# Attention and a two-layer feed-forward block on one core: other issue costs for SyncE in the planner, and a limit by due time on its second engines

## The chip, the cores and the metric

One core of a Trainium2 chip runs the whole program. The metric is the device time of one execution in microseconds (us); lower is better. The engines are PE (TensorE, matmuls), DVE (VectorE), ACT (ScalarE), POOL (GpSimd) and SP (SyncE, which here issues every DMA).

## The reference

Causal attention over 4 batches, 12 heads, 448 positions and head size 64, followed by two dense layers with an ELU between them. The weights arrive as 64-bit floats.

```python
scores = scale * np.matmul(q, k.transpose(0, 1, 3, 2))
scores = np.where(mask, -1000000000.0, scores)
attn = np.exp(scores - np.max(scores, axis=-1, keepdims=True))
attn = attn / (np.sum(attn, axis=-1, keepdims=True) + 1e-09)
x = np.matmul(attn, v)            # 1792 tokens x 768 after the heads are joined
h = x @ w_in                      # 768 -> 2048
g = np.where(h > 0.0, h, np.exp(np.minimum(h, 0.0)) - 1.0)
out = g @ w_out                   # 2048 -> 768
```

## The kernel before, in words

**Tiling.** Tokens are cut into four groups of 448 columns: position block c (112 positions) of each of the four batches. `layers(0)` and `layers(1)` compute the first dense layer for groups 0 and 1, `mixed_o(0)` the second layer for both, then `mixed_h` and `mixed_o(1)` the two layers for groups 2 and 3. The attention for group 1 (`attention(0)`) and for groups 2 and 3 (`attention(1)`) is woven into the first three of these. From `mixed_o(0)` on each matrix product is done as seven half-size products (numbered 1, 2, 6, 7, 4, 5, 3 in the order of `GROUPS`), each of whose operands are sums or differences of blocks: `halves` makes the activations' (products 6 and later, function `add`, L693), `mixed` the weights'. Each float32 operand goes to TensorE as a high and a low part, three matmuls for a product (`three`, L727 to L729): `hi_lo` makes the high part (ACT L685, or DVE L686 as a second engine) and the low part by a subtraction (L688: DVE, or POOL as a second engine).

**The planner.** Nothing is issued while the work is described. `plan.add` records each piece of work with its buffers, and one or more "ways": (engine, cost in us, function, whether it uses the SBUF port that DVE and POOL share). The first way is the preferred engine, any other is a second engine. PE work gets a due time as it is described; `Plan.run` carries due times back through successors and through the buffers that are to be reused. Then it simulates: at each step every ready piece offers a start time `s` on each of its ways, the engine with the earliest start takes, among its pieces that could start within 0.12 us of that, the one due first, and its function is called. A port piece on one of DVE and POOL starts only when the other's port piece has ended. A second engine is passed over if the first engine would finish the piece before it ends there plus `LEAST` = 0.8 us. So the order of instructions on each engine, and the choice between engines, is fixed before the kernel runs, by the costs in the code. On the chip each engine then works through its list in that order, waiting on semaphores.

**DMA.** Every DMA is a piece on SP. Its cost is its issue time, 0.36 us up to 128 "rows" and 0.57 us above (L313); its landing is reckoned from the end of the issue by size and `LANDS` = 3.2 us. Work that reads the data becomes ready then.

**Lines that the steps touch.** L668 stores converted weights, L638 loads 64-bit weights (`load64`, for w_in and for w_out), L483 loads v, L843 loads half-size weights (`raw_piece`), L398 stores reciprocals. L646, L650, L651, L654 and L657 convert 64-bit weights, L657 on POOL alone. L335 is the softmax's maximum on DVE (`nm`), L339 its exponential on ACT, L593 the transposes on PE that need it. L815 adds on DVE what PE has left in PSUM.

Of the kernel before, what the change touches and what calls it, by code (L numbers as in the profile page):

```python
# [11 lines left out]
U32 = mybir.dt.uint32  # L12
# [5 lines left out]
CP = 112  # L18
# [90 lines left out]
class Plan:  # L109
# [7 lines left out]

    LANDS = 3.2

    def __init__(self):  # L120
        self.works, self.cap = [], 1e9

# [27 lines left out]
    def run(self):  # L150
        for n, w in enumerate(self.works):
            w.n = n
        for w in reversed(self.works):
            cost = w.ways[0][1]
            lead = 2.0 * cost + 0.4 + (8.0 + 2.0 * w.size if w.size else 0.0)
            dues = [s.due - lead for s in w.succs]
            least = min(dues, default=1e9) - self.AHEAD
            for x in w.bufs:
                if x.ring and not x.ring.in_order:
                    if x.n + x.ring.places < len(x.ring.bufs_of):  # L160
                        dues.append(x.ring.bufs_of[x.n + x.ring.places].due - lead)
                dues += [max(o.due - lead, least if x.ring.long else -1e9) for o in x.after]
            if w.due is None:
                w.due = min([w.cap] + dues)
            for x in w.bufs:
                x.due = min(x.due, w.due)
            w.missing = len(w.preds)
        free, ported = {}, {}
        backlog = {}
        moved = 0.0  # L170
        ready = {w: 0.0 for w in self.works if not w.missing}
        todo = len(self.works)
        self.log = []
        self.done = []
        while todo:
            starts = {}
            for w, t in ready.items():
                skip = {}
                for b in w.bufs:
                    if not b.placed:  # L180
                        f = b.ring.free_at(b, skip.get(b.ring, 0))
                        skip[b.ring] = skip.get(b.ring, 0) + 1
                        if f is None:
                            t = None
                            break
                        t = max(t, f + self.HOP)
                if t is None:
                    continue
                for way, (eng, cost, _, port) in enumerate(w.ways):
                    s = max(t, free.get(eng, 0.0))  # L190
                    if port:
                        s = max([s] + [f for e, f in ported.items() if e != eng])
                    if way:
                        e0, c0 = w.ways[0][:2]
                        before = sum(
                            o.ways[0][1] for o, to in ready.items()
                            if o is not w and o.ways[0][0] == e0 and o.due < w.due and to <= s
                        )
                        if max(t, free.get(e0, 0.0)) + before + c0 < s + cost + self.LEAST:
                            continue  # L200
                    starts.setdefault(eng, []).append((s, w.due, w.n, way, w))
            assert starts, "no work can start"
            eng, cands = min(starts.items(), key=lambda kv: min(kv[1])[0])
            s0 = min(cands)[0]
            s, _, _, way, w = min((c for c in cands if c[0] <= s0 + 0.12), key=lambda c: (c[1], c[2]))
            _, cost, fn, port = w.ways[way]
            if port:
                ported[eng] = s + cost
            for b in w.bufs:
                if not b.placed:  # L210
                    b.placed = True
                    b.ring.order.append(b)
                    b()
            free[eng], w.eng = s + cost, eng
            if w.size:
                moved = max(moved, s + cost) + w.size
                w.end = moved + self.LANDS
            else:
                w.end = s + cost
            self.log.append((s, w.end, eng, w.due, cost))  # L220
            self.done.append(w)
            fn()
            del ready[w]
            todo -= 1
            for b in w.bufs:
                b.left -= 1
                b.end = max(b.end, w.end)
            for o in w.succs:
                o.missing -= 1
                if not o.missing:  # L230
                    o.ready = max(
                        p.end + (0.0 if p.eng == o.ways[0][0] and not p.size else self.HOP) for p in o.preds
                    )
                    ready[o] = o.ready

# [2 lines left out]
def attention_moe_kernel(ctx, tc, qk, v, w_in, w_out, out):  # L238
# [68 lines left out]
    def pool(n, fn, rate=2.3e-3):  # L307
        return ("POOL", 0.1 + rate * n, fn, True)

    def dma(kb, rows, fn, reads, writes, least=0.0, store=False):  # L310
        size = rows * (15.7 + 39.2 * kb / rows) / 16.0e3
        call = (lambda: fn(nc.sync)) if store else fn
        plan.add(("SP", 0.36 if rows <= 128 else 0.57, call, False), reads, writes, size=max(least, size))  # L313

# [161 lines left out]
    def loads_23(p, b):  # L478
        n = 2 * CP + S
        raw, hl, t = new("w", [P, n], name="qk"), new("w6", [P, 2, n], F32R, "qkhl"), new("v", [CP, 2, NCH, D])  # L480
        src = qk[b, 2 * p:2 * p + 2].rearrange("h d t s -> (h d) (t s)")[:, 2 * CP:]
        dma(n // 2, P, lambda: nc.sync.dma_start(out=raw(), in_=src), [], [raw])
        dma(224, CP, lambda: nc.sync.dma_start(out=t(), in_=v[b, p]), [], [t])  # L483
        hi_lo(lambda: hl()[:, 0], lambda: hl()[:, 1], raw, n, (hl, 0), (hl, 1), raw)
        done(raw)
        return [dict(
            reads=[hl], v=(t, lambda half, x: t()[:, half, x]), split=((0, 0), (0, 1), (1, 0)),
            q=lambda d, i, g=g: hl()[d, i, chunk(g)], k=lambda d, i, n: hl()[d, i, 2 * CP:2 * CP + n],
        ) for g in range(2)]
# [140 lines left out]
    def load64(key):  # L630
        r = words[key] = new("w6", [P, KT, P, 2], U32, "w64")
        if key[0] == "i":
            n, out, src = KT, lambda: r().rearrange("p k c w -> p k (c w)"), w_in[key[1]]
        else:
            x, n = key[2], 4
            out = lambda: r()[:, :n].rearrange("p (h k) c w -> p h k (c w)", h=2)
            src = w_out[key[1]].rearrange("p (h f) c -> p h f c", h=2)[:, :, 2 * x:2 * x + 2]
        dma(n * P, P, lambda: nc.sync.dma_start(out=out(), in_=src.bitcast(U32)), [], [r])  # L638

    def convert(key):  # L640
        r, w = words.pop(key), new("w", [P, KT, P])
        n = KT if key[0] == "i" else 4
        size = n * P
        low, high = (lambda: r()[:, :n, :, 0]), (lambda: r()[:, :n, :, 1])
        wf = lambda: w()[:, :n]
        plan.add(dve(size, lambda: nc.vector.tensor_scalar(  # L646
            wf(), f32(high()), MOST, -MOST, op0=ALU.min, op1=ALU.max
        ), 0.55e-3, 0.06, True), [(r, 1)], [w])

        plan.add(act(size, lambda: nc.scalar.activation(wf(), wf(), AF.Prelu, scale=REBIAS, alpha=2.0 ** 32), 0.09), [], [w])  # L650
        plan.add(dve(size, lambda: nc.vector.tensor_scalar(  # L651
            wf().bitcast(U32), wf().bitcast(U32), 3, None, op0=ALU.logical_shift_left
        ), 0.55e-3, 0.06, True), [], [w])
        plan.add(act(size, lambda: nc.scalar.activation(  # L654
            low().bitcast(I32), low(), AF.Copy, scale=2.0 ** -29
        ), 0.16), [], [(r, 0)])
        plan.add(pool(size, lambda: nc.gpsimd.tensor_tensor(  # L657
            out=wf().bitcast(I32), in0=wf().bitcast(I32), in1=low().bitcast(I32), op=ALU.add
        )), [(r, 0)], [w])
        if key[0] == "i":  # L660
            done(r)
            home, src = kin[key[1]], wf
        else:
            h = key[1] // HALF_E
            home = kout[key[1]].rearrange("p (h f) c -> p h f c", h=2)[:, h:, 2 * key[2]:2 * key[2] + 2]
            src = lambda: wf().rearrange("p (h f) c -> p h f c", h=2)[:, h:]
        k = kept[key] = Buf(None, lambda: home)
        dma(n * 64, P, lambda eng: eng.dma_start(out=home, in_=src()), [w], [k], store=True)  # L668
        return w if key[0] == "i" else (w, r)

    def fetch(f):
# [168 lines left out]

    def raw_piece(srcs, reads, dst):
        w = new("w", [P, KT, P])
        dma(KT * 64, 2 * P, lambda: nc.sync.dma_start(out=dst(w()), in_=srcs), reads, [w])  # L843
        return in_two(w, KT)

    GROUPS = ((1, 2), (6, 7, 4), (5, 3))
# [265 lines left out]
```

## Time and profile before

| | us |
|---|---|
| median of 3 runs | 625.55 (623.75 to 629.59) |
| profiled execution, its own time | 623.13 |
| span in the profile | 621.4 |
| PE busy | 600.4 (97%) |
| DVE busy | 508.5 (82%) |
| ACT busy | 425.9 (69%) |
| POOL busy | 163.2 (26%) |

Busy shares are means over the whole span. The time from the first to the last instruction is the span; the profiled execution's own time is 1.7 us longer. A line such as L688 belongs to a helper that many callers use; the tile names beside it (out<-in) tell them apart: `whl` are the weights' two parts, `ph`/`pl` the activations' parts in the half-size products, `G` the first layer's output, `u`, `s` and `t` intermediate rows, `nm` the softmax maximum.

### The profile page before, as it was taken

How to read it: one execution, taken by the hardware profiler on the slowest of the kernel's cores; microseconds unless marked ns; L12 is line 12 of the kernel's file. 1: busy time of each engine (PE TensorE's matmuls, PEld its weight loads, DVE VectorE, ACT ScalarE, POOL GpSimd, SP SyncE). 2: the span in 40 equal slices, each digit the busy share in tenths (PEclk: the TensorE clock that was granted, in tenths of full speed). 3: DMA queues.
4: the chain of work that ended last, by engine and by line, in shares of the span. 5: the costliest groups of instructions: out<-in, count | busy, mean ns of one | idle time of the engine just before them, and what ended most of it. 6: DMA issues, size and time to landing. Idle time of an engine off the chain costs nothing.

```text
span 621.4 us, 11699 instructions
## 1 busy us (share of the span) xinstructions
PE 600.4 (97%) x4056; PEld 514.9 (83%) x4056; DVE 508.5 (82%) x1126; ACT 425.9 (69%) x960; POOL 163.2 (26%) x116
## 2 busy tenths in 40 slices
PE   5999999998999999999999999999999999999997
PEld 5655688877788888788788878999999889999996
DVE  4897788689998998989998798597678999998611
ACT  6988889878899989786688684365446765573300
POOL 0235532144343445242220610030001352010000
PEclk9999999998999999999999999999999999999999
DMA  9999999877999999888868598864332343352111
GB/s 218 292 355 360 386 287 271 230 224 247 297 342 344 372 308 300 282 266 261 260 214 268 195 291 243 240 171 127 107 116 84 101 126 104 104 151 69 39 51 45
DMA packets 114172, 135.95 MB, mean 219 GB/s; under 512 B 42560, under 2 KB 86848, under 8 KB 114112
## 3 DMA queue, kind: packets, MB, share of 16 engines
q1 hardware_dynamic: 114112, 135.20, 71.2%
q8 instruction: 32, 0.52, 0.4%
q14 instruction: 28, 0.23, 0.1%
HBM read 103.02 MB, written 32.15 MB: 218 GB/s over the span
## 4 chain that ended last, share of the span: by engine, by line
PE 56%; DVE 15%; ACT 10%; DMA 9%; issue 6%; POOL 2%; SPq 1%; POOLq 0%; DVEq 0%; ACTq 0%
PE op L727 9%; PE op L728 8%; PE op L729 8%; PE hp L727 6%; PE hp L729 5%; PE hp L728 5%; PE hp L749 5%; ACT a L339 4%; PE av L561 3%; PE sc L528 3%; DMA R<-rdram 3%; DMA w<-in_w_out 2%; DVE whl L688 2%; DVE a L335 2%; PE tr L593 2%
## 5 line engine op out<-in xcount | busy, mean ns | idle before, releaser
L685 ACT ACTIVATE whl<-w 128x768 fp32r<-128x768 f32 x90 | 75.6, 842 | 76.8 <-PE op L729 41.4
L727 PE MATMUL op<-ph,whl 128*128 128x448 f32 x336 | 126.6, 377 | 0.0
L728 PE MATMUL op<-pl,whl 128*128 128x448 f32 x336 | 122.8, 365 | 0.0
L729 PE MATMUL op<-ph,whl 128*128 128x448 f32 x336 | 122.7, 365 | 0.0
L688 DVE TENSOR_TENSOR whl<-w,whl 128x768 fp32r<-128x768 f32 x102 | 105.1, 1031 | 20.1 <-ACT whl L685 19.4
L339 ACT ACTIVATE a<-a,nm 112x448 f32<-112x448 f32 (+3 forms) x192 | 97.7, 520 | 28.4 <-DVE nm L335 27.9
L657 POOL TENSOR_TENSOR w<-w,w 128x512 int32<-128x512 int32 (+1 forms) x40 | 67.2, 1683 | 134.7 <-DVE w L651 76.5
L335 DVE CUSTOM_DVE_ANT_0 a<-sc,mask 112x448 f32<-112x448 f32 (+3 forms) x192 | 74.0, 442 | 11.9 <-PE sc L429 7.9
L727 PEld LDWEIGHTS op<-ph,whl 128*128 128x128 f32 x336 | 63.2, 188 | 8.6 <-issue 3.8
L729 PEld LDWEIGHTS op<-ph,whl 128*128 128x128 f32 x336 | 63.1, 188 | 5.1
L728 PEld LDWEIGHTS op<-pl,whl 128*128 128x128 f32 x336 | 63.3, 188 | 4.3
L727 PE MATMUL hp<-ph,whl 128*128 128x448 f32 x168 | 61.7, 367 | 1.4 <-DVE u L815 1.3
L729 PE MATMUL hp<-ph,whl 128*128 128x448 f32 x168 | 61.4, 365 | 0.0
L728 PE MATMUL hp<-pl,whl 128*128 128x448 f32 x168 | 61.3, 365 | 0.0
L597 ACT ACTIVATE at<-tr 112x448 f32<-112x448 f32 (+1 forms) x120 | 53.1, 496 | 5.9 <-PE tr L593 5.9
L727 PE MATMUL hp<-xh,whl 128*128 128x448 f32 x144 | 57.0, 396 | 0.0
L593 PE MATMUL tr<-ident,a 112*112 112x112 f32 x432 | 52.2, 262 | 4.3 <-DVE nm L335 4.3
L593 PEld LDWEIGHTS tr<-ident,a 112*112 112x112 f32 x432 | 45.8, 134 | 12.1 <-DVE nm L335 6.2
L729 PE MATMUL hp<-xh,whl 128*128 128x448 f32 x144 | 53.4, 371 | 0.9 <-DVE whl L688 0.8
L728 PE MATMUL hp<-xl,whl 128*128 128x448 f32 x144 | 53.1, 369 | 0.8 <-DVE xl L688 0.8
L561 PEld LDWEIGHTS av<-at,v 112*64 112x64 f32 x864 | 43.0, 137 | 12.1 <-ACT at L597 5.7
L561 PE MATMUL av<-at,v 112*64 112x112 f32 x864 | 50.9, 264 | 1.1 <-ACT at L597 0.8
(111 smaller groups left out, 1102.2 us busy)
## 6 DMA issues: line engine op xcount, KB each, us to landing
w<-kin SPq DMA_DIRECT2D x44, 384.0 KB, 5.8
w<-in_w_in SPq DMA_DIRECT2D x16, 768.0 KB, 8.3
w<-in_w_out SPq DMA_DIRECT2D x24, 512.0 KB, 6.7
w<-sout SPq DMA_DIRECT2D x32, 384.0 KB, 3.6
w<-kout SPq DMA_DIRECT2D x24, 384.0 KB, 4.5
qk<-in_qk SPq DMA_DIRECT2D x24, 336.0 KB, 5.9
kin<-w SPq DMA_DIRECT2D x16, 384.0 KB, 7.9
sout<-w SPq DMA_DIRECT2D x12, 512.0 KB, 6.9
```

The lines of the kernel that those rows point to most:

```text
L335: plan.add(dve(n, lambda: nc.vector.tensor_tensor_reduce(out=a()[:, c], in0=sc()[:, c], in1=mask[:, S - n:], op0=ALU.add, op1=ALU.min, sca ...
L339: plan.add(act(n, lambda: nc.scalar.activation(a()[:, c], a()[:, c], AF.Exp, bias=nm()[:, x:x + 1], scale=-1.0, accum_out=su()[:, x:x + 1] ...
L561: nc.tensor.matmul(av()[half_of(half), chunk(u % 4)], o["v"][1](half, i), at()[:, chunk(x)], start=i == 0, stop=i == chunks(u) - 1,)
L593: nc.tensor.transpose(tr()[:, chunk(x)], a[:, chunk(i)], ident)
L597: act(w, lambda: nc.scalar.activation(at()[:, :w], tr()[:, :w], AF.Copy)),
L657: plan.add(pool(size, lambda: nc.gpsimd.tensor_tensor(out=wf().bitcast(I32), in0=wf().bitcast(I32), in1=low().bitcast(I32), op=ALU.add)), ...
L685: act(n, lambda: nc.scalar.activation(h(), x(), AF.Copy), 0.09),
L688: sub = lambda eng: lambda: eng.tensor_tensor(out=l(), in0=x(), in1=f32(h()), op=ALU.subtract)
L727: nc.tensor.matmul(acc(), wh(k), xh(), start=first, stop=False, skip_group_check=more)
L728: nc.tensor.matmul(acc(), wh(k), xl(), start=False, stop=False, skip_group_check=more)
L729: nc.tensor.matmul(acc(), wl(k), xh(), start=False, stop=last, skip_group_check=more)
L749: pe(ONE, lambda: nc.tensor.matmul(hp(), w[0]()[:, k], x(), start=k == 0, stop=k == KT - 1), [*w, x], [hp], due)
```

## The change

The planner's cost of a DMA on SP becomes 0.48 us or 0.66 us, by a flag `long` (without it, more than 128 rows). Three callers set it so that a DMA of up to 128 rows counts as long (v at L483, w_out at L638, the stores of w_out's half at L668), and `raw_piece` so that one of 256 rows counts as short. Second engines get a new condition: a second engine isn't offered a piece of work that is due more than `SOON` = 20 us after the start it would have. One expression is broken into two lines.

```diff
+    SOON = 20.0
...
                     if port:
                         s = max([s] + [f for e, f in ported.items() if e != eng])
+                    if way and w.due > s + self.SOON:
+                        continue
                     if way:
...
-    def dma(kb, rows, fn, reads, writes, least=0.0, store=False):
+    def dma(kb, rows, fn, reads, writes, least=0.0, store=False, long=None):
         size = rows * (15.7 + 39.2 * kb / rows) / 16.0e3
         call = (lambda: fn(nc.sync)) if store else fn
-        plan.add(("SP", 0.36 if rows <= 128 else 0.57, call, False), reads, writes, size=max(least, size))
+        plan.add(("SP", 0.66 if (rows > P if long is None else long) else 0.48, call, False), reads, writes, size=max(least, size))
...
-        dma(224, CP, lambda: nc.sync.dma_start(out=t(), in_=v[b, p]), [], [t])
+        dma(224, CP, lambda: nc.sync.dma_start(out=t(), in_=v[b, p]), [], [t], long=True)
...
-        dma(n * P, P, lambda: nc.sync.dma_start(out=out(), in_=src.bitcast(U32)), [], [r])
+        dma(n * P, P, lambda: nc.sync.dma_start(out=out(), in_=src.bitcast(U32)), [], [r], long=key[0] == "o")
...
-        dma(n * 64, P, lambda eng: eng.dma_start(out=home, in_=src()), [w], [k], store=True)
+        dma(n * 64, P, lambda eng: eng.dma_start(out=home, in_=src()), [w], [k], store=True, long=key[0] == "o")
...
-        dma(KT * 64, 2 * P, lambda: nc.sync.dma_start(out=dst(w()), in_=srcs), reads, [w])
+        dma(KT * 64, 2 * P, lambda: nc.sync.dma_start(out=dst(w()), in_=srcs), reads, [w], long=False)
```

## Rows read from the trace of the kernel before

**Rows 1.** By stretch: busy us on PE, PEld, DVE, ACT, POOL; clock, DMA.
```profile
120.00:383.00 263.00, 255.91 (x2048) 218.33 (x2043) 238.97 (x532) 213.41 (x494) 95.16 (x65) 0.99 0.88 278
...
480.00:560.00 80.00, 78.60 (x387) 71.94 (x386) 78.25 (x121) 53.07 (x98) 21.53 (x15) 1.00 0.41 118
560.00:622.00 62.00, 57.07 (x282) 52.56 (x280) 26.51 (x43) 10.51 (x16) 0.00 (x0) 1.00 0.17 47
```

**Rows 2.** What PE waited for: total us, times, longest.
```profile
PE tr L593 <- DVE nm L335: 4.3, 4, 2.2
...
PE hp L727 <- DVE u L815: 1.3, 1, 1.3
PE hp L728 <- DVE xl L688: 0.8, 1, 0.8
PE av L561 <- ACT at L597: 0.8, 1, 0.8
PE hp L729 <- DVE whl L688: 0.8, 1, 0.8
```

**Rows 3.** PE in order of time: start, us, what [idle before <-releaser].
```profile
150.15 0.93 PE L593 MATMUL tr<-ident,a 112*112 112x112 f32 x6 [2.24 <-DVE nm L335]
```

**Rows 4.** The two stretches behind that idle time; columns as in rows 1.
```profile
150.00:152.00 2.00, 1.85 (x11) 1.49 (x12) 2.00 (x9) 1.87 (x7) 0.00 (x0) 0.80 1.07 311
152.00:156.00 4.00, 4.00 (x20) 3.50 (x21) 4.00 (x7) 3.23 (x9) 2.74 (x2) 0.67 0.86 270
```

**Rows 5.** DVE in order of time, ahead of that idle time's end.
```profile
145.87 1.38 DVE L688 TENSOR_TENSOR whl<-w,whl 128x768 fp32r<-128x768 f32 x1
147.17 1.37 DVE L693 TENSOR_TENSOR w<-w 128x256 f32<-128x256 f32 x1
148.57 0.43 DVE L693 TENSOR_TENSOR w<-w,w 128x256 f32<-128x256 f32 x1
```

**Rows 6.** POOL in order of time, the same stretch.
```profile
145.13 3.13 POOL L688 TENSOR_TENSOR pl<-G,ph 128x448 fp32r<-128x448 f32 x2
```

**Rows 7.** Line 727: duration min/median/max ns, first and last start us.
```profile
L727 PE MATMUL op<-ph,whl x336: 362/365/493, 244.5 to 616.3; 128*128 128x448 f32 x168
L727 PE MATMUL hp<-ph,whl x168: 362/365/472, 410.6 to 514.2; 128*128 128x448 f32 x168
```

**Rows 8.** Lines 688 and 693 on POOL: durations, first and last start, as rows 7.
```profile
L688 POOL TENSOR_TENSOR pl<-G,ph x10: 1140/1482/3059, 130.9 to 552.9; 128x448 fp32r<-128x448 f32 x10
...
L693 POOL TENSOR_TENSOR G<-G x9: 1142/1265/1873, 171.7 to 266.7; 128x448 f32<-128x448 f32 x9
L693 POOL TENSOR_TENSOR G<-u,G x6: 1154/1158/1802, 492.5 to 519.4; 128x448 f32<-128x448 f32 x6
L693 POOL TENSOR_TENSOR u<-u x4: 1167/1640/1748, 497.1 to 507.0; 128x448 f32<-128x448 f32 x4
```

**Rows 9.** Groups on DVE by shape: the same subtraction there.
```profile
L693 DVE TENSOR_TENSOR u<-u 128x448 f32<-128x448 f32 x4 | 2.5, 617 | 0.0
```

**Rows 10.** DVE in order of time, around PE's wait for u.
```profile
495.15 0.94 DVE L688 TENSOR_TENSOR whl<-w,whl 128x768 fp32r<-128x768 f32 x1
...
501.55 1.59 DVE L688 TENSOR_TENSOR whl<-w,whl 128x768 fp32r<-128x768 f32 x1
503.06 0.61 DVE L815 TENSOR_TENSOR u<-hp,u 128x448 f32<-128x448 f32 x1
```

**Rows 11.** POOL in order of time, the same stretch.
```profile
501.17 1.16 POOL L693 TENSOR_TENSOR G<-u,G 128x448 f32<-128x448 f32 x1 [1.43 <-DVE u L822]
502.40 1.74 POOL L693 TENSOR_TENSOR u<-u 128x448 f32<-128x448 f32 x1
```

**Rows 12.** SP's issues by line: duration min/median/max ns, first and last start.
```profile
L638 SPq DMA_DIRECT2D w<-in_w_out x24: 540/580/739, 81.6 to 217.6; - x24
L843 SPq DMA_DIRECT2D w<-sout x32: 319/320/598, 261.0 to 565.5; - x32
```

**Rows 13.** A wait of DVE for a DMA: total us, times, longest.
```profile
DVE w L646 <- DMA w<-in_w_out: 0.6, 1, 0.6
```

More of the change, by code (lines that the diff above doesn't have):

```diff
@@ L231, in run @@
                     o.ready = max(
-                        p.end + (0.0 if p.eng == o.ways[0][0] and not p.size else self.HOP) for p in o.preds
+                        p.end + (0.0 if p.eng == o.ways[0][0] and not p.size else self.HOP)
+                        for p in o.preds
                     )
```

## The prediction, made blind

> **What bounds the kernel now.** I read the busy time by stretch first. From 120 to 383 us PE is busy 255.91 of 263.00 us, from 480 to 560 us 78.60 of 80.00 [rows 1]: PE sets the time, its matmuls are the same in number after the change, so all that can be won is the time in which PE stands still or runs slowly. Next comes the list of what PE waited for [rows 2]. The reader is to see two things in it. Nearly all of these waits end on DVE: four for the softmax maximum `nm` (4.3 us, the longest 2.2), one for `u` (1.3), one each for a low part `xl` and a weight's low part `whl` (0.8 each), and one on ACT's `at` (0.8). They sum to 8.0 us. The list's other rows are waits of the first pairs at the start; behind it, no wait of PE ends on a DMA. The list in order of time puts the longest, 2.24 us, in front of the transposes at 150.15 us [rows 3]. It costs twice: after PE had stood idle the granted clock was 0.80 of full for 2 us and 0.67 for the next 4 [rows 4], where its two levels are 2.4 and 1.2 GHz. The work lost is 2 x 0.20 + 4 x 0.33 = 1.7 us. So 8.0 + 1.7 = 9.7 us is all that lies open to a better order behind the start.
>
> Why was `nm` late? DVE has no time to spare in these stretches: 238.97 of 263.00 us busy, and 78.25 of 80.00 [rows 1]. Just ahead of the stall it took 1.38 us for a weight's low part and 1.37 us for a sum of 256 columns [rows 5], while POOL made two low parts `pl` in 3.13 us [rows 6]. The same sum of 256 columns took 0.43 us on DVE once POOL had ended [rows 5], and a weight's low part takes 0.94 us at another time [rows 10]. So POOL's 3.13 us cost DVE (1.38 - 0.94) + (1.37 - 0.43) = 1.38 us, and the softmax stands behind it in DVE's list. PE's wait for `u` looks alike: the weight's low part at 501.55 us took 1.59 us instead of 0.94, with `u`'s addition right behind it [rows 10], while POOL worked on `G` and `u` rows [rows 11].
>
> **The limit of 20 us on second engines.** What is taken away: POOL's pieces that aren't due yet. The two `pl` at 145 us feed `mixed_o(0)`, whose first matmul starts at 244.5 us [rows 7], some 100 us later. Of the ten `pl` that POOL makes from `G` the first starts at 130.9 us [rows 8]; it and the one behind it lie even earlier. The nine `G` differences [rows 8] feed product 6, the third of seven. By even shares between 244.5 and 410.6 us [rows 7] it would begin at 244.5 + 2/7 x 166.1 = 292 us (my estimate); they start between 171.7 and 266.7 us [rows 8]. The six `G` and four `u` differences [rows 8] start between 492.5 and 519.4 us; product 6 of `mixed_o(1)` begins, by the same share between 514.2 and 616.3 us [rows 7], at about 543 us. Due times lie some us ahead of use, so a few of the last are inside the limit and stay. I count 4 + 9 + 10 = 23 pieces; by the medians of their groups POOL spends 4 x 1.482 + 9 x 1.265 + 6 x 1.158 + 4 x 1.640 = 30.8 us on them [rows 8].
>
> What is added: those pieces go to DVE, or wait until they are due within 20 us and may go to POOL again. On DVE one takes 0.617 us [rows 9]: 23 x 0.617 = 14.2 us. Thirteen of them, 8.0 us, fall between 120 and 300 us, where DVE's idle time up to 383 us is 263.00 - 238.97 = 24.0 us [rows 1]. The planner takes the piece due first, so the far ones fill holes. The other ten, 6.2 us, meet 80.00 - 78.25 = 1.75 us of idle time; what doesn't fit is pushed into 560 to 622 us, where DVE has 62.00 - 26.51 = 35.5 us [rows 1], or to POOL once due. If that cover failed, 6.2 - 1.75 = 4.5 us would be late on DVE and, at worst, on PE.
>
> What is given back: at 145 us 3.13 us of POOL cost DVE 1.38 us, or 0.44 for each us. For the last ten pieces, 6 x 1.158 + 4 x 1.640 = 13.5 us of POOL [rows 8], that is 5.9 us, about the 6.2 us that they cost. DVE's total thus hardly changes; what changes is that urgent work no longer stands behind far-off work. The terms: at 150 us the stall shrinks by 1.38 of 2.24 us, and the remaining 0.86 is the size of the 0.8 us waits; I take the slow clock of 1.7 us as gone with it: 3.1 us. At 503 us 0.65 us is given back by the one instruction that I can price, and the one before it in line was slowed too; I take the whole wait, 1.3 us, with 0.65 as the lower bound. The high parts that DVE makes as a second engine fall under the same limit and go back to ACT, which is busy 213.41 of 263.00 and 53.07 of 80.00 us [rows 1]; a term of nothing, covered by ACT's holes.
>
> The trace has DVE slowed but not stopped: 1.38 us lost in 3.13 us. The Trainium skill, GPSIMD Engine Reference, section Key points, says that GpSimd shares its SBUF interfaces with VectorE and contends with its instructions that have two SBUF inputs; if DVE stood still for all of POOL's time, 3.13 us would come back instead of 1.38, which is more than the whole stall of 2.24 us, and the term would be 2.24 + 1.7 = 3.9 us instead of 3.1. The row decides; the rest does not use it.
>
> **The issue costs.** A w_out load takes SP 0.580 us where the plan had 0.36, and a half-size weight load 0.320 where it had 0.57 [rows 12]; the new 0.66 and 0.48 lie above both, by 0.08 and 0.16 us, and put the two forms in the right order. SP adds nothing to its own work by this: the same DMAs are issued. The change acts through the order: consumers of a load are set later, by up to 0.30 us for a w_out load and by the sum of the rises of those issued ahead of it. What that can save is what engines waited for loads that came later than planned: 0.6 us for a w_out load on DVE [rows 13]; PE's waits behind the start have none [rows 2]. What it can cost, from below by nothing and from above by about the waits that stand in the list now, is a new order with its own lateness: 8.0 us [rows 2]. Between saving 0.6 and costing 8.0 the trace's nearest rows are waits of 0.8 us, one of which may come or go; I take 0.
>
> **The sum.** 623.13 us of the profiled execution - 3.1 - 1.3 = 618.7 us. The median of the runs shown is 625.55, 2.4 us above that execution, so on the scale of the median I forecast 618.7 + 2.4 = 621.1, say 621 us.
>
> **Rivals.**
> 1. *More goes than I count.* The other waits vanish too: 8.0 - 2.24 - 1.3 = 4.5 us, and the remaining 0.86 at 150 us counts among the same kind. 621 - 4.5 = 616.5 us. For it: all but one of them end on DVE. Against it: the pieces beside them on POOL may be near due, and those stay.
> 2. *New waits for old.* A planner's new order moves all of DVE, ACT and SP, and with DVE at 91% and 98% of its stretches a wait of 0.8 to 2.2 us is made as easily as lost. With 4.4 us won and lost again: 623 to 627, middle 625.5 us. For it: the kernel's waits are short, many and spread. Against it: the two largest have one named cause.
> 3. *DVE becomes the bound, slower.* Place: 480 to 560 us, with DVE at 78.25 of 80.00. POOL's far-off help is refused, the ten pieces stay on DVE and the 20 us that are left once they count as due are too few; weights' low parts come late, PE waits 4.5 us, and the clock falls as at 150 us, 1.7 us for each such wait, for two of them 3.4. With nothing won elsewhere: 625.5 + 4.5 + 3.4 = 633.4 us. It decides once DVE's backlog in that stretch passes what POOL can take in 20 us, 20 / 1.35 = 15 pieces (13.5 us for ten) [rows 8]; I count ten.
> 4. *The limit hardly bites*, since due times are earlier than I reckon: then both terms are nothing and the time is about 625 us. It goes with rival 2 in the chances.
>
> **How the numbers follow.** Forecast (618 to 624 us) 0.45; rival 1 0.15; rivals 2 and 4 0.25; rival 3 0.15. The range that leaves out 2 in 10 drops the far half of rival 1 and most of rival 3: 614 to 630 us. About 1% is what a measurement of this kernel can tell from no change, and 1% of 625.55 is 6.3 us: faster means under 619.3, which takes rival 1 and a quarter of the forecast's chance, 0.15 + 0.12 = 0.27. Slower means over 631.8: most of rival 3, 0.13, and a tail of rival 2, 0.02, so 0.15. The rest, 0.58, is within 1%.
>
> **What would show it.** Right: POOL's groups of `G` and `u` differences are gone or start within some 30 us of use, DVE has more L693 and fewer L686, PE's waits for `nm` sum to under 3 us, and no stretch from 120 us on has a granted clock under 0.95. The issue costs alone show as the same SP durations in another order. Wrong: the same sum of PE's waits in other places (rival 2), PE waits for `whl` or `pl` between 500 and 600 us (rival 3), or a wait of PE for a load behind the start, which no row of before has.

## The result, and the profile after

The changed kernel takes 618.35 us in the median (616.93 to 618.93, 4 runs), against 625.83 us (4 runs) for the kernel before. The ratio is 0.9884, with a 95% interval of 0.9847 to 0.992: 1.2% faster. Its profiled execution took 618.64 us. That of the kernel before took 623.13 us, 2.7 us under the median of 625.83; the traces thus explain a difference of 4.5 us, and what the longer executions of the kernel before add, up to the 7.5 us between the medians, stands in no trace.

The page of the changed kernel begins with its span and the busy time of each engine (share of the span, instructions):

```profile
span 616.9 us, 11714 instructions
...
PE 599.2 (97%) x4056; PEld 516.2 (84%) x4056; DVE 498.1 (81%) x1143; ACT 451.8 (73%) x1002; POOL 73.9 (12%) x57
```

POOL went from 163.2 to 73.9 us. What is left on it, by group and shape (count, busy us, mean ns, idle before), is nearly all L662, which is L657 of before:

```profile
L662 POOL TENSOR_TENSOR w<-w,w 128x512 int32<-128x512 int32 x24 | 37.3, 1556 | 94.6 <-DVE w L656 31.7 <-ACT w L659 23.8 <-DMA rdram<-tt 12.4
L662 POOL TENSOR_TENSOR w<-w,w 128x768 int32<-128x768 int32 x16 | 31.0, 1946 | 65.1 <-DVE w L656 35.2 <-DMA w<-in_w_out 6.7 <-DMA q<-in_qk 5.7
L698 POOL TENSOR_TENSOR w<-w,w 128x256 f32<-128x256 f32 x2 | 1.5, 734 | 2.4 <-DVE w L698 2.4
L698 POOL TENSOR_TENSOR w<-w 128x256 f32<-128x256 f32 x2 | 1.5, 732 | 0.0
L693 POOL TENSOR_TENSOR xl<-xs,xh 128x448 fp32r<-128x448 f32 x1 | 1.3, 1337 | 0.8 <-ACT xh L690 0.8
```

Five optional pieces stayed on POOL, where the profile of before has 64. High parts on DVE fell as well, from 45 casts to two; the 43 that went to ACT took 23.0 us of DVE before. DVE is less busy, 498.1 us in place of 508.5, with 59 more subtractions and sums.

What PE waited for in the changed kernel (total us, times, longest):

```profile
PE sc L434 <- DMA k<-in_qk: 5.1, 2, 4.5
PE hp L734 <- DVE whl L693: 2.7, 4, 1.6
PE hp L732 <- ACT whl L690: 2.3, 2, 1.2
PE av L372 <- ACT at L362: 1.6, 1, 1.6
PE tr L598 <- DVE nm L340: 0.5, 1, 0.5
PE rb L454 <- DVE rr L350: 0.5, 1, 0.5
PE hp L733 <- POOL xl L693: 0.4, 1, 0.4
PE av L566 <- ACT at L602: 0.3, 1, 0.3
```

The first, the fourth and the sixth row belong to the start. The rest sum to 6.2 us, where [rows 2] has 8.0, and all of them lie before 250 us: asked for 250 to 620 us alone, the list is empty. Before, that stretch held 4.1 us of them (`nm` 2.0, `u` 1.3, `at` 0.8). The stretches show the same (busy us of PE, PEld, DVE, ACT, POOL, then granted clock and DMA), to be laid beside [rows 1]:

```profile
120.00:383.00 263.00, 256.73 (x2077) 220.10 (x2076) 239.88 (x563) 221.52 (x511) 38.84 (x27) 0.99 0.89 282
...
480.00:560.00 80.00, 80.00 (x397) 74.15 (x396) 79.06 (x134) 58.76 (x103) 0.00 (x0) 1.00 0.42 119
560.00:622.00 62.00, 52.57 (x260) 48.39 (x258) 20.71 (x32) 10.13 (x16) 0.00 (x0) 0.98 0.14 40
```

From 480 to 560 us PE now never stands still, with DVE at 79.06 of 80.00 us: DVE is as full as before, but nothing urgent is late.

Where the time came from is read best from the first matmul of the second layer. Line 732 (727 of before), with the first and the last start in us:

```profile
L732 PE MATMUL op<-ph,whl x336: 362/365/492, 248.2 to 611.8; 128*128 128x448 f32 x168
L732 PE MATMUL hp<-ph,whl x168: 362/365/369, 408.1 to 509.7; 128*128 128x448 f32 x168
```

In [rows 7] the `op` matmuls start between 244.5 and 616.3 us, 371.8 us apart; here they are 363.6 us apart. So 8.2 us were won behind that point and 248.2 - 244.5 = 3.7 us lost ahead of it, together the 4.5 us between the spans. (Eight transposes of about 0.1 us each lie behind that point here and ahead of it in the kernel before. On the same work the two figures are thus about 9.0 and 4.5 us.) In the text below "the second half" is this stretch, from the first to the last `op` matmul of the first of the three lines.

### The profile page after: what moved, and what is told of

Same layout as the page of the kernel before. It is cut to its first block, busy times and chain, and to the rows that moved or that the text cites. A ratio compares the mean times of both kernels' runs of the same rounds, so it can differ in the third digit from the quotient of the medians.

```text
span 616.9 us, 11714 instructions
## 1 busy us (share of the span) xinstructions
PE 599.2 (97%) x4056; PEld 516.2 (84%) x4056; DVE 498.1 (81%) x1143; ACT 451.8 (73%) x1002; POOL 73.9 (12%) x57
## 4 chain that ended last, share of the span: by engine, by line
PE 62%; DVE 2%; DMA 2%; ACT 1%; issue 1%; SPq 0%; ACTq 0%; DVEq 0%
PE op L732 12%; PE op L733 11%; PE op L734 11%; PE hp L734 6%; PE hp L732 6%; PE hp L733 6%; PE av L566 4%; PE tr L598 3%; PE sc L533 3%; DMA w<-kin 2%; ACT whl L690 0%; DVE G L698 0%; DVE G L827 0%; DVE w L698 0%; DVE a L340 0%
## 5 line engine op out<-in xcount | busy, mean ns | idle before, releaser
L690 ACT ACTIVATE whl<-w 128x768 fp32r<-128x768 f32 x107 | 89.7, 842 | 70.6 <-PE op L734 40.9
L693 DVE TENSOR_TENSOR whl<-w,whl 128x768 fp32r<-128x768 f32 x108 | 103.2, 958 | 24.1 <-ACT whl L690 23.0
L662 POOL TENSOR_TENSOR w<-w,w 128x512 int32<-128x512 int32 (+1 forms) x40 | 68.3, 1712 | 159.8 <-DVE w L656 67.0
L340 DVE CUSTOM_DVE_ANT_0 a<-sc,mask 112x448 f32<-112x448 f32 (+3 forms) x192 | 73.9, 444 | 10.3 <-PE sc L434 8.3
L566 PE MATMUL av<-at,v 112*64 112x112 f32 x864 | 49.0, 263 | 0.3 <-ACT at L602 0.3
```

The costliest lines, as they stand in the source:

```text
L340: plan.add(dve(n, lambda: nc.vector.tensor_tensor_reduce(out=a()[:, c], in0=sc()[:, c], in1=mask[:, S - n:], op0=ALU.add, op1=ALU.min, sca ...
L566: nc.tensor.matmul(av()[half_of(half), chunk(u % 4)], o["v"][1](half, i), at()[:, chunk(x)], start=i == 0, stop=i == chunks(u) - 1,)
L662: plan.add(pool(size, lambda: nc.gpsimd.tensor_tensor(out=wf().bitcast(I32), in0=wf().bitcast(I32), in1=low().bitcast(I32), op=ALU.add)), ...
L690: act(n, lambda: nc.scalar.activation(h(), x(), AF.Copy), 0.09),
L693: sub = lambda eng: lambda: eng.tensor_tensor(out=l(), in0=x(), in1=f32(h()), op=ALU.subtract)
```

## The experiments

Theory A: the limit brings the gain, and within it (A1) because POOL's work slows DVE, or (A2) because the high parts left DVE. Theory B: the issue costs bring it. Theory C: any new order of the planner moves the time by as much. Each kernel was compared with the kernel before on its own chip. "Second half" and POOL's busy time are those of its profiled execution. Where the expectations count 52 and 27 optional pieces on POOL, pieces of one kind in a row are counted once; by the profiles they are 64 and 31.

| kernel | median us | ratio to before (95%) | POOL busy us | second half us |
|---|---|---|---|---|
| before | 625.8 | | 163.2 | 371.8 |
| changed | 618.35 | 0.9884 (0.9847 to 0.992) | 73.9 | 363.6 |
| limit alone | 617.68 | 0.9882 (0.9855 to 0.9908) | 77.1 | 363.5 |
| issue costs alone | 630.18 | 1.0063 (1.0036 to 1.009) | 149.8 | 375.7 |
| issue costs alone, + 0.01 us | 623.33 | 0.9972 (0.9943 to 1.0001) | 151.3 | 371.0 |
| before, SP costs + 0.01 us | 624.51 | 0.998 (0.9956 to 1.0003) | 163.9 | 366.3 |
| changed, SP costs + 0.01 us | 617.09 | 0.9875 (0.9832 to 0.9917) | 75.4 | 363.5 |
| before, no optional work on POOL | 618.86 | 0.9894 (0.9866 to 0.9923) | 70.1 | 363.4 |
| before, no high parts on DVE | 624.84 | 1.0002 (0.9976 to 1.0027) | 162.0 | 368.0 |
| changed, no second engines | 617.96 | 0.9886 (0.9855 to 0.9917) | 68.0 | 364.5 |
| changed, POOL repeats 320 columns | 629.14 | 1.0057 (1.0028 to 1.0086) | 182.6 | 373.6 |
| changed, POOL repeats 8 columns | 615.67 | 0.9828 (0.9793 to 0.9863) | 110.6 | 363.7 |
| changed, limit at 40 us | 625.08 | 1.0001 (0.9973 to 1.003) | 112.6 | 368.1 |
| changed, attention spread to 212 | 620.60 | 0.9932 (0.9907 to 0.9957) | 75.4 | 368.8 |

**Which part of the change.** The limit with the old costs:

```diff
-        plan.add(("SP", 0.66 if (rows > P if long is None else long) else 0.48, call, False), ...
+        plan.add(("SP", 0.36 if rows <= 128 else 0.57, call, False), ...
```

> The limit of 20 us on second engines, with the old issue costs. Theory A (the limit brings the gain, the issue costs nothing): ratio to before 0.985 to 0.992, POOL keeps fewer than 10 of its 52 optional pieces, PE has no wait of over 0.5 us behind 250 us. Theory B (the issue costs bring it): ratio 0.997 to 1.003. Theory C (any new order of the planner moves the time by as much, the gain is luck): a ratio anywhere from 0.985 to 1.015.

The ratio was 0.9882, and its list of PE's waits from 252 us on is empty. That is the whole gain of the change. The new costs without the limit:

```diff
-                    if way and w.due > s + self.SOON:
-                        continue
```

> The new issue costs alone, second engines without the limit. Theory A: ratio to before 0.996 to 1.004, POOL's optional pieces about as many as before, and the waits of PE for the softmax maximum still there behind 250 us. Theory B: ratio 0.985 to 0.992. Theory C: anywhere from 0.985 to 1.015.

The ratio was 1.0063: neither theory A nor B expected a loss. The next two kernels, and later a third, size what a meaningless change of the order does:

```diff
-        plan.add(("SP", 0.36 if rows <= 128 else 0.57, call, False), ...
+        plan.add(("SP", 0.37 if rows <= 128 else 0.58, call, False), ...
```

> The kernel before with SP's costs moved by 0.01 us (0.37 and 0.58): nothing that means anything, but the planner makes another order. It sizes theory C. Theory A: within 0.4% of before, ratio 0.996 to 1.004, since what costs time is POOL's share of the work and that stays. Theory C: off by 0.8% or more on either side.

> The changed kernel with SP's costs moved by 0.01 us (0.67 and 0.49). Theory A: ratio to before within 0.4% of the changed kernel's, 0.984 to 0.993, and again no waits of PE of over 0.5 us behind 250 us. Theory C: off by 0.8% or more from it on either side.

> The new issue costs alone, without the limit, moved by 0.01 us (0.67 and 0.49). If the costs themselves lose time without the limit: ratio to before 1.003 to 1.010 as with the costs alone. If that loss was one unlucky order: 0.995 to 1.003.

Moving SP's costs by 0.01 us gave 0.998 from the kernel before, 0.9875 from the changed one, and 0.9972 from the costs alone. So the loss of the costs alone is not owed to the costs as such, which neither win nor lose anything that these runs can tell. Theory C reaches as far as the step from 630.18 to 623.33 us, 1.1% (in the profiled execution some 2 us of it are the slower matmuls of the last section, which need not come from the order), but only among kernels with POOL at work: of the kernels in which POOL has little beside L657 and the attention is where it was, none is over 618.86 us, and of those in which it streams more none is under 623.33.

**POOL's work or the high parts.** The kernel before without any optional work on POOL, and without high parts on DVE:

```diff
-        plan.add([dve(n, sub(nc.vector), port=True), pool(n, sub(nc.gpsimd))], [tx, th], [tl])
+        plan.add([dve(n, sub(nc.vector), port=True)], [tx, th], [tl])
...
-        plan.add([dve(n, two(nc.vector), port=True), pool(n, two(nc.gpsimd))], reads, writes)
+        plan.add([dve(n, two(nc.vector), port=True)], reads, writes)
```

> The kernel before, old issue costs and no limit, but subtractions and sums have DVE as their only engine: POOL keeps L657 alone, DVE still makes high parts as a second engine. Theory A1 (what the limit won is that POOL no longer slows DVE): ratio to before 0.985 to 0.992. Theory A2 (it is that high parts left DVE for ACT): 0.997 to 1.003.

```diff
             act(n, lambda: nc.scalar.activation(h(), x(), AF.Copy), 0.09),
-            dve(n, lambda: nc.vector.tensor_copy(h(), x()), 0.55e-3, 0.06, True),
```

> The kernel before, old issue costs and no limit, but high parts have ACT as their only engine; POOL still takes subtractions and sums. Theory A1: ratio to before 0.997 to 1.005. Theory A2: 0.985 to 0.992.

0.9894 and 1.0002: A1, and not A2. The page and line 727 of the kernel without optional work on POOL:

```profile
PE 596.1 (97%) x4056; PEld 512.3 (83%) x4056; DVE 517.6 (84%) x1182; ACT 432.0 (70%) x968; POOL 70.1 (11%) x52
...
L727 PE MATMUL op<-ph,whl x336: 362/365/492, 247.2 to 610.6; 128*128 128x448 f32 x168
```

DVE took over all 64 pieces, 163.2 - 70.1 = 93.1 us of POOL's time, and its busy time rose from 508.5 to 517.6, by 9.1 us alone. Eight casts, worth 5.7 us, left DVE for ACT in this kernel; by the means of their shapes in it the 64 pieces take DVE 43.4 us (my estimate). So the rest of DVE's work became 43.4 - 5.7 - 9.1 = 28.6 us shorter: two thirds of the help that POOL gave were taken back by slowing DVE.

**Is it the slowing itself?** In the changed kernel, POOL repeats every second low part of 448 columns into a tile that nobody reads. The order on DVE is the same. The control has the same instructions and waits with 8 columns in place of 320:

```diff
+    scratch, twice = const.tile([P, 320], F32, name="scratch"), [0]
...
+        def low():
+            sub(nc.vector)()
+            twice[0] += n == S
+            if n == S and twice[0] % 2 == 0:
+                nc.gpsimd.tensor_tensor(out=scratch, in0=x()[:, :320], in1=f32(h())[:, :320], op=ALU.subtract)
-        plan.add([dve(n, sub(nc.vector), port=True), pool(n, sub(nc.gpsimd))], [tx, th], [tl])
+        plan.add([dve(n, low, port=True), pool(n, sub(nc.gpsimd))], [tx, th], [tl])
```

> The changed kernel, with the same order on DVE, ACT, PE and SP, but POOL repeats every second low part that DVE makes of 448 columns (320 columns of it) into a scratch tile that nobody reads: work that takes nothing off DVE. Theory A1 by the slowing of DVE alone: POOL's some 70 us of extra work at 0.44 us of DVE for each us cost DVE 30 us, waits of PE for DVE come back and the ratio to before is 0.995 to 1.02. If instead the gain is only a better order: 0.985 to 0.992, as the changed kernel.

> The control to the run in which POOL repeats low parts: the same instructions on POOL with the same waits and the same buffers read, but 8 columns of each in place of 320. If POOL's repeated work cost time by slowing DVE while it streams: ratio to before 0.984 to 0.992, as the changed kernel. If it cost time because POOL's reads hold buffers longer or add waits: 0.997 to 1.010, as with 320 columns.

With 320 columns all the gain is gone (1.0057), with 8 columns it is all there (0.9828, a little below the 0.984 to 0.992 that was expected). Groups on DVE by shape and the engines of the page, first with 320 columns:

```profile
PE 604.4 (97%) x4056; PEld 515.0 (82%) x4056; DVE 530.3 (85%) x1143; ACT 451.1 (72%) x1002; POOL 182.6 (29%) x129
...
L695 DVE TENSOR_TENSOR whl<-w,whl 128x768 fp32r<-128x768 f32 x108 | 110.3, 1025 | 9.6 <-ACT whl L692 8.7
L695 DVE TENSOR_TENSOR pl<-G,ph 128x448 fp32r<-128x448 f32 x64 | 47.5, 756 | 0.8 <-ACT ph L692 0.8
L342 DVE CUSTOM_DVE_ANT_0 a<-sc,mask 112x448 f32<-112x448 f32 x48 | 27.9, 615 | 0.2 <-PE sc L535 0.2
```

then with 8:

```profile
PE 597.5 (97%) x4056; PEld 515.5 (84%) x4056; DVE 499.1 (81%) x1143; ACT 451.3 (74%) x1002; POOL 110.6 (18%) x129
...
L695 DVE TENSOR_TENSOR whl<-w,whl 128x768 fp32r<-128x768 f32 x108 | 102.9, 956 | 22.4 <-ACT whl L692 21.3
L695 DVE TENSOR_TENSOR pl<-G,ph 128x448 fp32r<-128x448 f32 x64 | 38.4, 614 | 0.9 <-ACT ph L692 0.9
L342 DVE CUSTOM_DVE_ANT_0 a<-sc,mask 112x448 f32<-112x448 f32 x48 | 27.9, 615 | 1.9 <-PE sc L535 1.9
```

The reader is to compare the mean durations: a low part of `G` takes DVE 756 ns in the kernel with 320 columns and 614 ns in that with 8, while the softmax maximum, which reads `sc` in PSUM, takes 615 ns in both. The two kernels have the same number of POOL instructions; POOL's busy time differs by 182.6 - 110.6 = 72.0 us and DVE's by 530.3 - 499.1 = 31.2 us, 0.43 us of DVE for each us of POOL. (Against the changed kernel's 73.9 and 498.1 us it is 32.2 us for 108.7, or 0.30; but 36.7 us of that POOL time is there with 8 columns too, where DVE pays 1.0 us.) Single pairs show how it happens, two of the kernel with 320 columns, then one stretch of that with 8 (start, us):

```profile
571.42 1.15 POOL L700 TENSOR_TENSOR scratch<-G,ph 128x320 f32<-128x320 f32 x1
571.75 1.63 DVE L695 TENSOR_TENSOR whl<-w,whl 128x768 fp32r<-128x768 f32 x1
...
574.21 1.14 POOL L700 TENSOR_TENSOR scratch<-u,ph 128x320 f32<-128x320 f32 x1
574.54 1.29 DVE L695 TENSOR_TENSOR pl<-u,ph 128x448 fp32r<-128x448 f32 x1
```

```profile
556.42 2.80 POOL L700 TENSOR_TENSOR scratch<-G,ph 128x8 f32<-128x8 f32 x1 [2.60 <-ACT ph L692]
556.95 1.15 DVE L695 TENSOR_TENSOR pl<-u,ph 128x448 fp32r<-128x448 f32 x2
558.02 1.15 DVE L695 TENSOR_TENSOR pl<-G,ph 128x448 fp32r<-128x448 f32 x2
```

In the pairs POOL ends at 572.57 and 575.35 us and DVE 0.81 and 0.48 us later, where DVE's instructions take 0.94 and 0.61 us undisturbed: nearly all of DVE's work was done after POOL had ended. In the last stretch it is POOL that waits: its 8 columns take 2.80 us, until DVE's run of subtractions ends. In these rows the two engines take turns.

The control's reads are shorter as well, so it does not by itself rule out that 320 columns cost time by holding buffers longer. ACT did wait for these reads, 6.4 us in all, but ahead of 549.75 and 567.38 us, where PE makes 100 matmuls in each 20 us, against 101 in the changed kernel; so that is not where the time went. And PE's waits for DVE and ACT come back behind 250 us (250 to 520 us, the kernel with 320 columns; with 8 columns the list from 246 us is empty):

```profile
PE hp L739 <- DVE u L827: 1.5, 1, 1.5
PE av L568 <- ACT at L604: 1.5, 3, 0.8
```

**How the limit works.** Second engines refused altogether, and the limit at 40 us:

```diff
-                    if way and w.due > s + self.SOON:
+                    if way:
```

> The changed kernel with every second engine refused (no limit by due time, simply never). If the limit of 20 us matters only because it refuses nearly everything: ratio to before 0.984 to 0.992, as the changed kernel. If the five pieces on POOL and the two casts on DVE that it still lets through are needed: over 0.992, with waits of PE for low or high parts between 120 and 250 us longer than the changed kernel's 6 us.

```diff
-    SOON = 20.0
+    SOON = 40.0
```

> The changed kernel with the limit at 40 us in place of 20. It lets 27 optional pieces on POOL where 20 us lets 5 and no limit 52. Theory A1 (POOL's work slows DVE): between the two, ratio to before 0.990 to 0.999, with waits of PE for DVE or ACT back behind 250 us. If the limit matters only by keeping far-off work away: as the changed kernel, 0.984 to 0.991.

Refusing everything gives 0.9886, so the due time as such does no work here: at 20 us the limit nearly switches the second engines off. At 40 us, with 31 optional pieces on POOL, the gain is gone, 1.0001. Theory A1 had expected something between, 0.990 to 0.999; the interval touches that but the median misses it. Waits of PE from 249 us on are between the two, as expected, and the second half is too (368.1 us). How much is lost doesn't follow from the amount of POOL's work alone, though: the kernel before with SP's costs moved by 0.01 us has 163.9 us of it and a second half of 366.3 us. The waits at 40 us:

```profile
PE tr L598 <- DVE nm L340: 1.0, 1, 1.0
PE av L566 <- ACT at L602: 0.5, 1, 0.5
```

The rest of its time went ahead of the first `op` matmul, which starts at 249.3 us, and there the kernels differ with no pattern that I found: with POOL at work that start is at 244.5 to 251.4 us, without at 244.1 to 248.2.

**A version that beats both?** The remaining waits lie between 120 and 250 us, so DVE's load there was thinned out:

```diff
-    SPREAD = ((0.0, 64.0), (64.0, 200.0))
+    SPREAD = ((0.0, 64.0), (64.0, 212.0))
```

> The changed kernel with the second part of the attention spread to 212 us of matmul work in place of 200. If DVE's density between 120 and 250 us is what makes the remaining waits of PE for weights' low parts and ACT's high parts: 2 to 4 us less, ratio to before 0.980 to 0.986. If these waits have other causes: as the changed kernel, 0.986 to 0.992.

It gave 0.9932, outside both ranges, so the expectation fell and nothing was won; whether it is slower than the changed kernel isn't shown, since the intervals (0.9907 to 0.9957 and 0.9847 to 0.992) overlap. Its second half holds more of the attention and can't be laid beside the others. The control with 8 columns has the lowest time, 615.67 us. Its interval (0.9793 to 0.9863) overlaps that of the changed kernel as well, so it isn't shown that it beats it.

## Why the prediction was right or wrong

**The direction and the time.** 621 us was forecast, 618.35 measured, within 614 to 630. The likeliest class, within 1%, was not met by a little: the ratio is 0.9884, its interval reaches to 0.992. For the profiled execution 618.7 us was forecast and 618.64 measured; most of the 2.7 us by which the median came out lower is the 2.4 us by which I set it above that execution. The changed kernel's median lies 0.3 us below it. That the sum came out so near is luck: the largest term, 3.1 us at 150 us, hardly came, and about as much came from waits that I had not summed. Behind 250 us all waits on the list went, as in rival 1; ahead of it they grew from 3.9 to 6.2 us, as in rival 2. Of the signs that I named, `G` and `u` differences are gone from POOL and the waits for `nm` sum to 0.5 us, but the granted clock did fall under 0.95 once more.

**What bounds the kernel.** Right: PE sets the time, and the waits that could go ended on DVE. That DVE's low parts take longer while POOL works is what the runs with 320 and 8 columns show.

**How many pieces are refused.** Mis-sized: I counted 23 by the distance between their start and their first use, and the change took 59 of 64 away. The limit of 40 us lets 26 more through than 20 us, among them weights' low parts and `qkhl`, which I had not counted as far off; 33 more are refused at 40 us too. The planner runs farther ahead of its own due times than I read from the trace.

**The stall at 150 us, 3.1 us.** Wrong: it stayed. PE in order of time in the changed kernel [idle before <-releaser], and the stretch behind it:

```profile
148.53 1.57 PE L598 MATMUL tr<-ident,a 112*112 112x112 f32 x11 [0.54 <-DVE nm L340]
151.25 0.47 PE L732 MATMUL hp<-xh,whl 128*128 128x448 f32 x1 [1.15 <-ACT whl L690]
...
152.24 0.74 PE L734 MATMUL hp<-xh,whl 128*128 128x448 f32 x1 [0.32 <-DVE whl L693]
```

```profile
152.00:156.00 4.00, 3.76 (x12) 3.12 (x14) 4.00 (x8) 4.00 (x13) 1.41 (x1) 0.57 0.54 125
```

The wait for `nm` did shrink, from 2.24 us [rows 3] to 0.54, but the weight's high part, now on ACT alone, is 1.15 us late and its low part 0.32: 2.0 us in all. The granted clock fell as before, to 0.57 for 4 us, 4 x 0.43 = 1.7 us, against 1.7 from [rows 4]. So of the 3.1 us some 0.2 came. The step that failed is that the place of the largest wait was taken to be free once its cause went; the next engine in line, ACT, was late behind it. I had put the high parts' move to ACT at nothing, covered by its holes; from 150 to 156 us ACT has none, and over the kernel PE waits 2.3 us for high parts from ACT where [rows 2] has no such wait. That ACT was late because of the move is argued, not shown: the limit alone moves the high parts as well, and there PE stands still at 184 us (1.6 us for ACT's high part) and not at 150, while with no second engines at all no wait for a high part is on the list.

**The wait for `u` at 503 us, 1.3 us.** Right, in mechanism and size. DVE in the changed kernel, against [rows 10]:

```profile
502.42 0.95 DVE L693 TENSOR_TENSOR whl<-w,whl 128x768 fp32r<-128x768 f32 x1
503.29 0.63 DVE L820 TENSOR_TENSOR hp<-hp,u 128x448 f32<-128x448 f32 x1
```

The weight's low part takes 0.95 us in place of 1.59, and PE no longer waits.

**Where the rest came from.** On the same work 9.0 us came in the second half. The list of what PE's matmuls waited for names 4.1 us of it, as rival 1 had it for all waits behind 250 us. Most of the rest lies in time in which the profile has PE busy, and is found in the waits of PE's weight loads (PEld: total us, times, longest, in the second half), first before, then changed:

```profile
PEld av L561 <- ACT at L597: 5.1, 15, 1.0
PEld op L727 <- issue: 3.8, 12, 0.3
PEld tr L593 <- DVE nm L335: 3.4, 4, 1.5
PEld hp L727 <- DVE u L815: 2.4, 3, 1.7
```

```profile
PEld op L732 <- issue: 3.8, 12, 0.3
PEld av L566 <- ACT at L602: 1.8, 6, 0.3
PEld av L566 <- ACT ph L690: 1.2, 4, 0.3
```

All rows of `av`, `tr` and `hp` sum to 12.4 us before and 4.2 us after: 8.2 of the 9.0 us. (They hold the 4.1 us and are not added to them.) The waits for `at` go back to DVE too: ACT's exponential, whose output is transposed and copied to `at`, waited 18.1 us for `nm` in this stretch and now waits 3.8. So the size that I missed is that of many short waits on the softmax's chain, which a list of the matmuls' waits does not show in full. Ahead of that half 3.7 us were lost, or 4.5 on the same work, which is within what orders differ by there.

**What DVE pays.** Right in size: I took 0.44 us of DVE for each us of POOL, and between 320 and 8 columns it is 0.43; over all 64 pieces it is 28.6 us for 93.1, or 0.31. The Trainium skill, GPSIMD Engine Reference, section Key points, names the shared interfaces as a cause of contention for instructions with two SBUF inputs. The runs agree (756 against 614 ns). But that DVE was "slowed but not stopped" misread the rows. In the pairs above it stands still until POOL's instruction ends, and POOL in its turn waits for DVE; so POOL's 3.13 us in [rows 6], where two such pieces take 2.28 us at their shortest [rows 8], hold waiting of its own, and DVE's loss is less than POOL's time. The sum does not use that sentence.

**The issue costs, a term of nothing.** Right by the kernels with and without them: 617.68 and 618.35 us under the limit.

**Rival 3.** It did not come: DVE is at 79.06 of 80.00 us from 480 to 560 us, and PE waits for nothing there. Its point of decision was DVE's backlog, and the 59 pieces went into what the 43 casts left free and into what DVE won by not being slowed. **Rival 4**, that the limit hardly bites, was the reverse of what happened.

## What to carry to other kernels

Before work is offloaded to a second engine, price it by what the first engine's total does: here 93.1 us of POOL's work saved DVE about 15 of 43 us and cost the kernel 1%. A repeat of the offloaded instruction into a scratch tile, once at full and once at tiny size, tells contention apart from order and waits, and pairs of instructions that overlap show whether one engine stops the other. Where matmuls seem busy, the weight loads' waits are worth reading too. A planner's result should be judged beside one or two meaningless changes of its costs, since 0.01 us on a cost went with a step of 1.1% in one kernel here.

## What the runs showed of the hardware that was not expected

In the profiled execution of the issue costs alone, the matmuls of the last stretch were 2% slower, at a granted clock of 1.00 (columns as above; the first stretch lies ahead of a wait of 1.3 us at 508 us, the others behind it):

```profile
480.00:500.00 20.00, 20.00 (x100) 18.44 (x99) 19.82 (x29) 16.37 (x31) 6.50 (x5) 1.00 0.28 92
540.00:560.00 20.00, 20.00 (x98) 18.18 (x97) 19.30 (x34) 12.76 (x24) 0.20 (x1) 1.00 0.53 148
580.00:600.00 20.00, 20.00 (x99) 18.16 (x98) 12.15 (x20) 6.09 (x9) 0.00 (x0) 1.00 0.13 36
```

PE is busy throughout in all three, with 100 matmuls in 20 us ahead of the wait and 98 and 99 behind it; the weight loads' busy time falls from 18.44 to 18.16 us with them. That kernel's seven runs lie at 626.1 and 627.1 us and between 630.0 and 631.4 us. Whether the slower ones are those with this pitch, and what sets it, was not tried.
